# Retention and MLP on one Trainium2 core: the second product of the first block, half of it by seven products, and k of chunks 4 to 7 by casting transfers

## The chip, the cores and the metric

The kernel runs on one core of one Trainium2 chip. The metric is device time in microseconds of one execution, the median of three timed runs. TensorE (PE) multiplies, VectorE (DVE), ScalarE (ACT) and GpSimd (POOL) do the elementwise work, SyncE (SP) issues most transfers; POOL and ACT can issue transfers too.

## The reference

Two layers follow each other: a retention recurrence over 4 batches, 8 heads, 768 tokens and 64 features per head, and a two-layer MLP with Mish on its 3072 tokens of 512 features.

```python
for t in range(S):
    state = gamma[None, :, None, None] * state + np.einsum('bhd,bhe->bhde', k[:, :, t], v[:, :, t])
    y[:, :, t] = scale * np.einsum('bhd,bhde->bhe', q[:, :, t], state)
...
h = x @ w_in                       # 3072 x 512 by 512 x 2048
sp = np.where(h > 20.0, h, np.log1p(np.exp(np.minimum(h, 20.0))))
g = h * np.tanh(sp)
return (g @ w_out).astype(np.float32)   # 3072 x 2048 by 2048 x 512
```

## The kernel before

**Chunks and blocks.** The recurrence is worked in 24 chunks of 128 tokens, six to a batch. For a chunk, PE turns q and k (`turn`, L383, or a transposing transfer, `turn_by_dma`, L363), multiplies them to scores (`scores`, L394), DVE masks them (`mask`, L404), PE adds the masked scores times v (`present`, L463) and the carried state times q (`past`, L457). The state's increment is k times v (`outer_wide`, L445, for chunk 4; `outer`, L411, after that). `y_two` (L506) does present, outer and past of the two chunks of a block, and ACT copies the result to fp16 (`xt`, L516), which is what the MLP of that block starts from. The first block has four chunks (0 to 3), the ten others two each.

**The MLP.** Per block, the first product gives h in PSUM, ACT applies Mish and writes g (fp16), the second product multiplies g by `w_out`. `w_out` comes in four slices of 4 x 128 rows (`FPS` = 4, slices 0 to 3), each 1 MB in fp32; it is cast to fp16 by `cast_wout` (L179). From block 2 on the second product is done by seven half-size products in place of eight (`seven`, L744): sums of g (`sums_a`, L607, and so on) against sums of `w_out` (`weight_sums`, L574, tiles `tmat`, four DVE operations for each half). Block 1 uses seven products in its first product alone. Block 0 uses plain products in both.

**The stage at hand.** `first_block` (L842) runs the recurrence of chunks 0 to 3, then the loop at L936: sixteen steps of the first product (`g1`, L524), then fourteen steps of the second (`g2_mm`, L551), each of which takes one 128-row part of `w_out` for all four token tiles into four PSUM banks (`o_tiles`), and two steps that close the banks (`g2_out`, L557). The dictionary `plan` (L923) hangs the other work on steps of that loop: casts of the `w_out` slices (slices 0, 1 and 2 on DVE, slice 3 on ACT), the recurrence of chunks 4 and 5 (`casts`, `turn`, `scores_one`, `outer_wide`), and `y_two(1)` ahead of the last closing step. `some_late` (L570) takes DVE operations off a list of sums that nothing waits for yet.

**Loads.** Transfers go out in the order of the program on SP's queue: the weights, then q and v of chunk 4, the last quarter of `w_out` in two halves (`load_last_wout`), then q, k and v chunk by chunk (`load_more`, L825; `load_to`). Three loads of chunks 4 and 5 (k of 4, q and v of 5) are issued by ACT instead. Up to chunk 7 (`BRING` = 8) k is loaded as fp32 and cast by ACT (`cast_k`, L346); from chunk 8 on `bring_k` (L340) has POOL issue a transfer that casts to fp16 on its way. POOL scales and casts q and v (`cast_q`, L335; `cast_v`, L350).

**Order.** The order on every engine is the order of the program text (`tc.manual_schedule()`); waits are placed where tiles depend on one another. `gate` (L360) is a one-column POOL copy that makes POOL wait for a tile. `mmps` is a pool of four PSUM banks for the products, `atps` one of two double banks for the recurrence.

Of the kernel before, what the change touches and what calls it, by code (L numbers as in the profile page):

```python
# [9 lines left out]
FP16 = mybir.dt.float16  # L10
# [6 lines left out]
def kernel(  # L17
# [107 lines left out]
    nsnap = [0]  # L125
    SEVEN, HALF_SEVEN = 2, 1
    nload, late = [0], []
    BRING = CPB + 4
    stores = []


# [1 line left out]
    def room(g):  # L133
        loaded[g] = [
            lpool.tile([P, H, D], FP32, name=nm + "f", tag=nm + "f", bufs=6 if nm == "v" else 4)
            if g < BRING or nm != "k" else None for nm in "qkv"]

    def load_one(g, n, queue):
        b, c = divmod(g, NCH)
        queue.dma_start(  # L140
            loaded[g][n], (q, k, v)[n][b, :, c * C:(c + 1) * C].rearrange("h p d -> p h d"))

    def load(g):
        room(g)
        for n in (0, 1, 2) if g < BRING else (0, 2):
            load_one(g, n, nc.sync)

    def load_to(g):
# [27 lines left out]
        eng.tensor_copy(t, src[:, :, half * (TB // 2):(half + 1) * (TB // 2)])  # L176
        wins[s, half] = t

    def cast_wout(s, on_act=False):  # L179
        src = wtmps.pop(("out", s))  # L180
        t = cpool.tile([P, FPS, d_model], FP16, name=f"wout{s}")
        if on_act:
            for f in range(0, FPS, 2):
                nc.scalar.copy(t[:, f:f + 2], src[:, f:f + 2])
        else:
            nc.vector.tensor_copy(t, src)
        wouts[s] = t

    def store(n):
        for _ in range(n):  # L190
# [155 lines left out]
    def cast_k(g):  # L346
        if g < BRING:
            nc.scalar.copy(room16(g)[1], loaded[g][1])

    def cast_v(g):  # L350
        if g < NCK:
            nc.gpsimd.tensor_tensor(  # L352
# [1 line left out]

    def casts(g):
        cast_q(g)
        cast_k(g)
        cast_v(g)

    def gate(x):  # L360
        nc.gpsimd.tensor_copy(gate_t, x)  # L361
# [21 lines left out]
    def turn(g):  # L383
# [7 lines left out]
        nc.vector.tensor_copy(qkt, t_ps)  # L391
        qkts[g] = (qkt[:, :HP], qkt[:, HP:])

    def scores(g):  # L394
# [45 lines left out]
    def state(g):  # L440
        state_sum(g)
        state_decay(g, nc.vector)
        spread_state(g)

    def outer_wide(g):  # L445
        _, k16, v16, _ = cast[g]
        u_ps = u_tile()[:, 0]
        for i in range(HP):
            nc.tensor.matmul(
                u_ps[:, i], k16[:, 2 * i:2 * i + 2], v16[:, 2 * i:2 * i + 2],  # L450
                start=True, stop=True)
        su = stp.tile([P, HP, P], FP32, name="su", bufs=1)
        nc.vector.tensor_tensor(su, u_ps, states[g - 1], op=ALU.add)
        states[g] = stp.tile([P, HP, P], FP16, name="st")
        nc.vector.tensor_tensor(states[g], su, gcm, op=ALU.mult)  # L455

    def past(g, y):  # L457
        st, qt = states[g - 1], qkts[g][0]
# [26 lines left out]
    def outer_state(g):  # L485
        outer(g, u_tile()[:, 0, :, :D])
        state(g)
# [36 lines left out]
    def g1(blk, u):  # L524
        nt = BLOCKS[blk] * C
        per = TB // nt
        h_ps = mmps.tile([P, per, nt], FP32, name="h_ps", tag="mm")
        for j in range(per):
            s, f = divmod(u * per + j, FPS)
            for bp in range(NBP):  # L530
                nc.tensor.matmul(
                    h_ps[:, j], win(s, f, bp), xt(blk, bp),
                    start=(bp == 0), stop=(bp == NBP - 1))
        mish(blk, u, h_ps)
# [35 lines left out]
    def some_late(n):  # L570
        for _ in range(min(n, len(late))):
            late.pop(0)()
# [21 lines left out]

    def room_for_more():
        n, hf = NFB // 2, d_model // 2
        tmats.extend(
            wstage.tile([P, 2, n, hf], FP16, name="tmat", tag="wt", bufs=4) for _ in range(2))

    def sum_views(blk, f=slice(None)):  # L600
        s = gsums[blk % 2]
# [42 lines left out]
    def g1_seven(blk, steps):  # L644
# [54 lines left out]
        def step(name):  # L699
            for fn, *args in steps.get(name, ()):  # L700
                fn(*args)
# [10 lines left out]
        mm(pe, s(1), t(1), True)  # L712
        m5 = snap(pe)
        mish_plain(1, 0, h0)
        step("u2")
        step("p6")
        h1 = plain(3, 0)
        mm(px, s(3), t(3))
# [123 lines left out]
    def first_block():  # L842
# [72 lines left out]
        for s in range(1, NSL):  # L915
# [4 lines left out]
            if s >= 2:  # L920
                some_late(4)
        room_for_sums()
        plan = {  # L923
            9: [(cast_wout, 0)],
            12: [(cast_wout, 1)],
            16: [(cast_wout, 2), (load_more,), (casts, CPB)],
            23: [(casts, CPB + 1), (cast_wout, 3, True)],
            24: [(turn, CPB)],
            25: [(scores_one, CPB)],
            27: [(turn, CPB + 1)],  # L930
            28: [(outer_wide, CPB), (casts, CPB + 2), (turn_and_load, CPB + 2), (cast_q, CPB + 3)],
            29: [(scores_one, CPB + 1)],
            31: [(y_two, 1)],
        }
        o_tiles = [None] * CPB
        for u in range(2, 2 * NFB):  # L936
            if u < NFB:
                g1(0, u)
            elif u < 2 * NFB - 2:
                w = u - NFB  # L940
                for t in range(CPB):
                    if w == 0:
                        o_tiles[t] = mmps.tile([P, d_model], FP32, name="o_ps", tag="mm")
                    g2_mm(o_tiles[t], 0, t, w)
            else:
                for t in range(CPB // 2) if u % 2 == 0 else range(CPB // 2, CPB):
                    for w in range(NFB - 2, NFB):
                        g2_mm(o_tiles[t], 0, t, w)
                    g2_out(o_tiles[t], 0, t, 1, on_act=t == CPB - 1)
            for fn, *args in plan.get(u + 1, ()):  # L950
                fn(*args)
            if u == NFB - 1:
                room_for_more()
                late.extend(weight_sums(0) + weight_sums(1))
            if NFB <= u < NFB + 5:
                some_late(1)
# [46 lines left out]
    def steps_of_half(blk):  # L1003
        a = first[blk] + 4
        return {
            "p2": [(gate_x, blk), (cast_v, a - 1), (bring_k, a)],
            "u2": [(cast_k, a - 1)],
            "p6": [(turn_and_load, a - 1), (some_late, 1)],
            "p7": [(cast_q, a), (some_late, 1)],
            "p4": [(cast_v, a), (bring_k, a + 1), (some_late, 1), (store, 2)],  # L1010
            "end": [(turn_and_load, a), (store, 2)],
        }

    def plan_of(blk):
        a = first[blk] + 4
        return {10: [(scores_two, blk + 1)],
                11: [(cast_q, a + 1)],
                12: [(outer_state, first[blk] + 2), (cast_v, a + 1), (bring_k, a + 2),
                     (turn_and_load, a + 1)],
                14: [(y_two, blk + 1)]}  # L1020

# [56 lines left out]
```

## Time and profile before

| what | value |
|---|---|
| median of 3 runs | 202.63 us (202.52 to 202.92) |
| the profiled execution | 203.19 us, of which the span is 201.3 us |
| PE busy in the span | 192.6 us (96%) |
| DVE, ACT, POOL busy | 138.7, 112.9, 76.9 us |
| granted TensorE clock | 1.00 throughout |
| blocks 2 to 10, each | about 14.6 us (68.0 to 82.6 us is one) |

The span is what the profile covers, from the first to the last instruction; the remaining 1.9 us lie around it. The median of the timed runs is 0.56 us under the profiled execution's own time, so a difference found in the profile is carried to the median, not an absolute time. PE is nearly always busy, so its share says little: what counts is in which stretches PE stands still, and behind what. The stretch that the change touches lies between the last matmul of the first product (32.6 us) and the first of block 1 (51.9 us).

### The profile page before, as it was taken

The page shows a single profiled execution, that of the slowest core. Times are in us where ns is not written, and L with a number is a line of the kernel's source. Part 1 is how long each engine was busy: PE and PEld are TensorE (multiplying, and loading weights), DVE is VectorE, ACT ScalarE, POOL GpSimd, SP SyncE. Part 2 cuts the span into 40 slices and gives each one's busy share as a digit, 9 for nine tenths or more (in the row PEclk, how much of TensorE's full clock was granted, in tenths as well). Part 3 has the DMA queues.
Part 4 walks back from the last instruction along what each step waited for, and adds up shares of the span by engine and source line. Part 5 has one row for each costly group of instructions (what it writes and reads, how often), then busy time and mean ns, then how long its engine had stood idle before and what let it go on. Part 6 is the DMA issues. An engine that isn't in the chain of part 4 may idle for free.

```text
span 201.3 us, 5579 instructions
## 1 busy us (share of the span) xinstructions
PE 192.6 (96%) x2307; PEld 151.6 (75%) x2307; DVE 138.7 (69%) x278; ACT 112.9 (56%) x213; POOL 76.9 (38%) x103
## 2 busy tenths in 40 slices
PE   6987999979999999999999999999999999999993
PEld 2355444445774788988988988988988988988982
DVE  2787594969746559569479587587498597597362
ACT  2462674151780495494584684685664675775750
POOL 7072000617553355645716527618606706100000
PEclk9999999999999999999999999999999999999999
DMA  5999999999989999999998997996999982200202
GB/s 173 301 313 356 384 386 306 265 258 196 156 90 248 254 183 231 179 153 189 136 195 174 196 152 125 187 164 141 192 173 131 168 135 53 107 0 32 77 29 78
DMA packets 95897, 36.57 MB, mean 182 GB/s; under 512 B 82304, under 2 KB 89984, under 8 KB 95872
## 3 DMA queue, kind: packets, MB, share of 16 engines
q1 hardware_dynamic: 75968, 33.30, 74.8%
q0 software_dynamic: 16640, 2.10, 16.5%
q10 hardware_dynamic: 3264, 0.82, 2.4%
q8 instruction: 18, 0.29, 0.6%
q14 instruction: 7, 0.06, 0.1%
HBM read 27.30 MB, written 6.29 MB: 167 GB/s over the span
## 4 chain that ended last, share of the span: by engine, by line
PE 78%; DMA 8%; DVE 8%; ACT 2%; issue 1%; SPq 0%; DVEq 0%
PE o_ps L764 27%; PE h_ps L690 18%; PE h_ps L666 16%; DMA wt<-in_moe_w_out_dram 6%; PE o_ps L553 4%; PE y_ps L469 3%; PE at L400 3%; PE y_ps L460 2%; DMA qfirst<-in_q_dram 2%; PE u_ps L415 1%; DVE tmat L585 1%; ACT xt L516 1%; PE h_ps L838 1%; DVE st L455 1%; DVE tmat L587 1%
## 5 line engine op out<-in xcount | busy, mean ns | idle before, releaser
L690 PE MATMUL h_ps<-xt,win 128*128 128x256 f16 x320 | 41.6, 273 | 0.0
L683 DVE TENSOR_TENSOR hsum<-h_ps,hsnap 128x512 f32<-128x512 f32 x30 | 19.8, 688 | 22.3 <-PE h_ps L666 20.0
L690 PEld LDWEIGHTS <-win 128*128 128x128 f16 x320 | 29.3, 98 | 3.6
L337 POOL TENSOR_TENSOR qk<-qf,qvs 128x512 f16<-128x512 f32 x20 | 21.5, 1077 | 25.8 <-DMA qf<-in_q_dram 25.7
L764 PEld LDWEIGHTS <-gsum 128*128 128x128 f16 x288 | 27.7, 98 | 3.2
L406 DVE TENSOR_TENSOR am<-at,tri 128x1024 f16<-128x1024 f32 x20 | 24.3, 1217 | 3.5 <-PE at L400 3.5
L352 POOL TENSOR_TENSOR v<-vf,qvs 128x512 f16<-128x512 f32 x20 | 23.5, 1173 | 5.1 <-DMA vf<-in_v_dram 5.1
L764 PE MATMUL o_ps<-tmat,gsum 128*128 128x256 f16 x216 | 25.1, 273 | 0.0
L677 ACT ACTIVATE g<-hsum 128x512 f16<-128x512 f32 x30 | 18.5, 631 | 11.0 <-DVE hsum L683 10.9
L697 ACT ACTIVATE g<-h_ps 128x512 f16<-128x512 f32 x40 | 23.0, 603 | 0.7 <-PE h_ps L690 0.6
L764 PEld LDWEIGHTS <-g 128*128 128x128 f16 x216 | 21.0, 98 | 2.5
L553 PE MATMUL o_ps<-wout,g 128*128 128x512 f16 x96 | 22.7, 379 | 0.0
L673 ACT COPY hsnap<-h_ps 128x512 f32<-128x512 f32 x30 | 16.4, 581 | 10.7 <-PE h_ps L666 10.6
L666 PEld LDWEIGHTS <-wsum 128*128 128x128 f16 x320 | 19.5, 98 | 0.5
L778 DVE TENSOR_TENSOR osb<-o_ps,snap 128x256 f32<-128x256 f32 x27 | 11.3, 419 | 11.6 <-PE o_ps L764 10.1
L361 POOL COPY gate<-gsum 128x1 f16<-128x1 f16 x8 | 1.4, 181 | 44.6 <-DVE gsum L738 44.6
L770 ACT COPY snap<-o_ps 128x256 f32<-128x256 f32 x27 | 10.1, 373 | 13.7 <-PE o_ps L764 13.4
L516 ACT CAST xt<-y_ps 128x1024 f16<-128x1024 f32 x10 | 10.1, 1012 | 13.5 <-PE y_ps L460 13.5
L764 PE MATMUL o_ps<-wout,g 128*128 128x256 f16 x144 | 17.2, 273 | 0.0
L666 PE MATMUL h_ps<-xsum,wsum 128*128 128x128 f16 x240 | 16.7, 219 | 0.0
L666 PEld LDWEIGHTS <-win 128*128 128x128 f16 x240 | 15.1, 98 | 1.7 <-issue 1.0
L438 ACT COPY stx<-stc 64x256 f16<-64x256 f16 x30 | 12.0, 400 | 7.5 <-DVE stc L424 5.5
(105 smaller groups left out, 296.9 us busy)
## 6 DMA issues: line engine op xcount, KB each, us to landing
vf<-in_v_dram SPq DMA_DIRECT2D x23, 256.0 KB, 5.7
out_dram<-osb SPq DMA_DIRECT2D x22, 256.0 KB, 5.2
qf<-in_q_dram SPq DMA_DIRECT2D x19, 256.0 KB, 5.0
wt<-in_moe_w_out_dram SPq DMA_DIRECT2D x3, 1024.0 KB, 9.3
wi<-in_moe_w_in_dram SPq DMA_DIRECT2D x4, 512.0 KB, 7.6
wi<-in_moe_w_in_dram SPq DMA_DIRECT2D x2, 1024.0 KB, 11.8
qk<-in_k_dram POOLq DMA_DIRECT2D x16, 128.0 KB, 5.6
kf<-in_k_dram SPq DMA_DIRECT2D x7, 256.0 KB, 5.9
```

The lines of the kernel that those rows point to most:

```text
L337: nc.gpsimd.tensor_tensor(room16(g)[0], loaded[g][0], qs.unsqueeze(2).broadcast_to((P, H, D)), op=ALU.mult)
L352: nc.gpsimd.tensor_tensor(room16(g)[2], loaded[g][2], vs.unsqueeze(2).broadcast_to((P, H, D)), op=ALU.mult)
L406: nc.vector.tensor_tensor(am, ats.pop(g), tri.unsqueeze(1).unsqueeze(1).broadcast_to((P, 2, HP, C)), op=ALU.mult)
L516: nc.scalar.copy(xts[blk][:, :, :2 * C], y_ps.rearrange("p i j c -> p i (j c)"))
L553: nc.tensor.matmul(o_ps, gts[blk, fb][:, t * P:(t + 1) * P], wouts[s][:, f, cols], start=(fb == 0), stop=(fb == NFB - 1))
L666: nc.tensor.matmul(h_ps[:, f], w(f, d), x(d), start=first and f == 0 and d == 0, stop=d == n - 1, skip_group_check=True)
L673: nc.scalar.copy(x, h_ps)
L677: nc.scalar.activation(gt[:, 2 * i * FPS:(2 * i + 1) * FPS, j * P:(j + 1) * P], h, AF.Mish, scale=inv_boost3)
L683: nc.vector.tensor_tensor(h, h_ps, x, op=ALU.add)
L690: nc.tensor.matmul(h_ps[:, j], win(s, 2 * half + j, bp), xt(blk, bp), start=bp == 0, stop=bp == NBP - 1)
L697: nc.scalar.activation(gt[:, fb:fb + 2], h_ps, AF.Mish, scale=inv_boost3)
L764: nc.tensor.matmul(o_ps, x(f), w(f), start=first and f == 0, stop=f == n - 1, skip_group_check=True)
```

## The change

The loop over sixteen second-product steps is replaced by a new function `first_g2`. It treats the tokens of block 0 as two pairs of tiles, and of the four slices of `w_out` it multiplies slices 0 and 2 by seven products in place of eight (with the sums of `weight_sums(0)`, now made here, and four sums of g in `gsum`), slices 1 and 3 plainly. Slice 3 comes last for all tiles (`end`). Accumulators of a pair share two PSUM banks; partial results are copied out by ACT (into `osb` and `snap`) while the bank goes on accumulating. Slice 2 is cast half by DVE and half by ACT, slice 3 by ACT as before; the copies of turned q and k (`turn`) move from DVE to ACT. `outer_wide` is split, its second DVE operation (`decay_wide`) placed after the mask of chunk 5.

`BRING` goes from 8 to 4: k of chunks 4 to 7 comes by `bring_k`, issued by POOL, and the ACT casts of k and the fp32 loads of k are gone. All q and v loads of chunks 4 and 5 are on SP, ahead of the last quarter of `w_out`.

```diff
-    BRING = CPB + 4
+    BRING = CPB
...
-    def cast_wout(s, on_act=False):
+    def cast_wout(s, on_act=0):
...
+        n = FPS - on_act
+        if n:
+            nc.vector.tensor_copy(t[:, :n], src[:, :n])
+        for f in range(n, FPS, 2):
+            nc.scalar.copy(t[:, f:f + 2], src[:, f:f + 2])
...
-        load_one(CPB, 0, nc.sync)
-        load_one(CPB, 2, nc.sync)
+        for g in (CPB, CPB + 1):
+            load_one(g, 0, nc.sync)
+            load_one(g, 2, nc.sync)
     def load_more():
-        load_one(CPB, 1, nc.scalar)
-        load_one(CPB + 1, 0, nc.scalar)
-        load_one(CPB + 1, 2, nc.scalar)
-        load_one(CPB + 1, 1, nc.sync)
         load_last_wout(0)
         load_last_wout(1)
...
+        plan = {9: [(cast_wout, 0), (room_for_more,), (bring_first,)],
+                10: [(some_late, 1)], 13: [(cast_wout, 1), (room_for_more,)], 16: [(load_more,)]}
+        late.extend(weight_sums(0) + weight_sums(1))
+        for u in range(2, NFB):
+            g1(0, u)
             for fn, *args in plan.get(u + 1, ()):
                 fn(*args)
+        first_g2()
...
+    def bring_first():
+        gate(wtmps["out", 1][:, 0, :1])
+        bring_k(CPB)
+        bring_k(CPB + 1)
+
+    def first_g2():
...
+        for p in pairs:
+            mm(px[p], a(p, 0, 0), b(0, 0), True)
+            nc.scalar.copy(osb[p][0][:, 0], px[p])
+        g_sum(1, g_part(0, 1), g_part(2, 1), ALU.add)
+        g_sum(2, the_sum(1), g_part(0, 0), sub)
+        for p in pairs:
+            mm(pz[p], a(p, 1, 1), b(1, 1))
+        for p in pairs:
+            mm(pe[p], sm(p, 1), t(1), True)
+            nc.scalar.copy(m5[p], pe[p])
+        cast_wout(2, FPS // 2)
+        some_late(1)
+        gate(tmats[0][:, 1, 0, :1])
+        casts(CPB)
+        bring_k(CPB + 2)
+        some_late(1)
+        g_sum(3, g_part(0, 0), g_part(0, 1), sub)
+        g_sum(4, g_part(2, 0), the_sum(2), sub)
+        some_late(1)
+        for p in pairs:
+            mm(pb[p], a(p, 0, 1), b(1, 0))
+        for p in pairs:
+            mm(pb[p], a(p, 0, 2), b(2, 0))
+        for p in pairs:
+            mm(pe[p], a(p, 0, 1), b(1, 1))
+        for p in pairs:
+            mm(px[p], sm(p, 2), t(2))
+            nc.scalar.copy(osb[p][0][:, 1], px[p])
+        turn(CPB, True)
+        for p in pairs:
+            mm(px[p], sm(p, 3), t(3))
+            nc.vector.tensor_tensor(osb[p][1][:, 1], px[p], m5[p], op=ALU.add)
+        casts(CPB + 1)
+        bring_k(CPB + 3)
+        for p in pairs:
+            mm(pe[p], sm(p, 4), b(2, 1))
+        scores_one(CPB)
+        turn(CPB + 1, True)
+        cast_wout(3, FPS)
+        for p in pairs:
+            mm(px[p], a(p, 1, 2), t(4))
+        for p in pairs:
+            mm(px[p], a(p, 1, 1), b(1, 0))
+        outer_wide(CPB)
+        casts(CPB + 2)
+        turn_and_load(CPB + 2)
+        cast_q(CPB + 3)
+        scores_one(CPB + 1)
+        decay_wide(CPB)
+
+        def end(p, i):
+            mm((t0, t1)[i][p], a(p, i, 3), lambda f: wouts[3][:, f], last=True)
+            if i == 0:
+                nc.vector.tensor_tensor(osb[p][0], t0[p], osb[p][0], op=ALU.add)
+            else:
+                nc.vector.tensor_tensor(osb[p][1][:, 1], pz[p], osb[p][1][:, 1], op=ALU.add)
+                nc.scalar.copy(osb[p][1][:, 0], px[p])
...
+        end(0, 0)
+        end(0, 1)
+        end(1, 0)
+        y_two(1)
+        end(1, 1)
```

In the shorthand of `first_g2`, `a(p, i, s)` is g of token tile 2p+i and slice s, `b(s, j)` column half j of slice s of `w_out`, `sm(p, i)` and `t(i)` the sums of g and of `w_out`; each `mm` is four matmuls of 256 columns (512 in `end`). `px` and `pz` are the halves of one PSUM tile of the pair (`t1`), `pb` and `pe` those of the other (`t0`).

More of the change, by code (lines that the diff above doesn't have):

```diff
@@ L135, in room @@
             lpool.tile([P, H, D], FP32, name=nm + "f", tag=nm + "f", bufs=6 if nm == "v" else 4)
-            if g < BRING or nm != "k" else None for nm in "qkv"]
+            if nm != "k" else None for nm in "qkv"]
     def load_one(g, n, queue):
@@ L144, in load @@
         room(g)
-        for n in (0, 1, 2) if g < BRING else (0, 2):
+        for n in (0, 2):
             load_one(g, n, nc.sync)
@@ L177, in cast_win @@
         wins[s, half] = t
-    def cast_wout(s, on_act=False):
+    def cast_wout(s, on_act=0):
         src = wtmps.pop(("out", s))
[L181 to L187, printed above, removed]
+        t = wouts[s] = cpool.tile([P, FPS, d_model], FP16, name=f"wout{s}")
+        n = FPS - on_act
[3 more added lines that the diff above has]
+            nc.scalar.copy(t[:, f:f + 2], src[:, f:f + 2])
     def store(n):
@@ L344, in bring_k @@
                 room16(g)[1], k[b, :, c * C:(c + 1) * C].rearrange("h p d -> p h d"))
-    def cast_k(g):
-        if g < BRING:
-            nc.scalar.copy(room16(g)[1], loaded[g][1])
     def cast_v(g):
@@ L356, in casts @@
         cast_q(g)
-        cast_k(g)
         cast_v(g)
@@ L381, in spin_wide, with turn @@
             tri.unsqueeze(1).broadcast_to((P, n, C)), start=True, stop=True)
-    def turn(g):
+    def turn(g, on_act=False):
         q16, k16 = cast[g][:2]
@@ L390, in turn @@
         qkt = qktp.tile([P, H, C], FP16, name="qkt", bufs=4)
-        nc.vector.tensor_copy(qkt, t_ps)
+        if on_act:
+            nc.scalar.copy(qkt, t_ps)
+        else:
+            nc.vector.tensor_copy(qkt, t_ps)
         qkts[g] = (qkt[:, :HP], qkt[:, HP:])
@@ L451, in outer_wide, with decay_wide @@
                 start=True, stop=True)
-        su = stp.tile([P, HP, P], FP32, name="su", bufs=1)
-        nc.vector.tensor_tensor(su, u_ps, states[g - 1], op=ALU.add)
+        sus[g] = stp.tile([P, HP, P], FP32, name="su", bufs=1)
+        nc.vector.tensor_tensor(sus[g], u_ps, states[g - 1], op=ALU.add)
+    def decay_wide(g):
         states[g] = stp.tile([P, HP, P], FP16, name="st")
-        nc.vector.tensor_tensor(states[g], su, gcm, op=ALU.mult)
+        nc.vector.tensor_tensor(states[g], sus.pop(g), gcm, op=ALU.mult)
     def past(g, y):
@@ L483, in u_tile @@
         return atps.tile([P, 2, HP, P], FP32, name="u_ps", tag="at")
-    def outer_state(g):
-        outer(g, u_tile()[:, 0, :, :D])
-        state(g)
     def handed_on(blk):
@@ L596, in room_for_more @@
         n, hf = NFB // 2, d_model // 2
-        tmats.extend(
-            wstage.tile([P, 2, n, hf], FP16, name="tmat", tag="wt", bufs=4) for _ in range(2))
+        tmats.append(wstage.tile([P, 2, n, hf], FP16, name="tmat", tag="wt", bufs=4))
     def sum_views(blk, f=slice(None)):
@@ L714, in g1_seven @@
         mish_plain(1, 0, h0)
-        step("u2")
         step("p6")
@@ L922, in first_block @@
         room_for_sums()
[L923 to L949, printed above, removed]
+        plan = {9: [(cast_wout, 0), (room_for_more,), (bring_first,)],
+                10: [(some_late, 1)], 13: [(cast_wout, 1), (room_for_more,)], 16: [(load_more,)]}
@@ L950, in first_block @@
+        late.extend(weight_sums(0) + weight_sums(1))
+        for u in range(2, NFB):
+            g1(0, u)
             for fn, *args in plan.get(u + 1, ()):
                 fn(*args)
[L952 to L956, printed above, removed]
-        hsnaps.append(gp.tile([P, 4, TB], FP32, name="hsnap", tag="g0"))
+        first_g2()
+        hsnaps.append(gp.tile([P, 4, TB], FP32, name="hsnap", tag="g0"))
@@ new lines, in bring_first, with a, sm, b @@
+    def bring_first():
[3 more added lines that the diff above has]
+    def first_g2():
+        hf = d_model // 2
+        sub = ALU.subtract
+        pairs = range(CPB // 2)
+        t1 = [mmps.tile([P, 2, hf], FP32, name="o_ps", tag="mm") for _ in pairs]
+        t0 = [mmps.tile([P, 2, hf], FP32, name="o_ps", tag="mm") for _ in pairs]
+        osb = [[op.tile([P, 2, hf], FP32, name="osb", tag="osb") for _ in range(2)] for _ in pairs]
+        m5 = [op.tile([P, hf], FP32, name="snap", tag="snap", bufs=3) for _ in pairs]
+        pb, pe = [t[:, 0] for t in t0], [t[:, 1] for t in t0]
+        px, pz = [t[:, 0] for t in t1], [t[:, 1] for t in t1]
+        sums = gsums[0].rearrange("p s (f a) t -> p s f (a t)", a=2)
+        def a(p, i, s):
+            return lambda f: gts[0, s * FPS + f][:, (2 * p + i) * P:(2 * p + i + 1) * P]
+        def sm(p, i):
+            return lambda f: sums[:, i - 1, f, p * P:(p + 1) * P]
+        def b(s, j):
+            return lambda f: wouts[s][:, f, j * hf:(j + 1) * hf]
+        def t(i):
+            return lambda f: tmats[(i - 1) // 2][:, (i - 1) % 2, f]
+        def mm(o_ps, x, w, first=False, last=False):
+            for f in range(FPS):
+                nc.tensor.matmul(
+                    o_ps, x(f), w(f), start=first and f == 0, stop=last and f == FPS - 1,
+                    skip_group_check=True)
+        def g_part(s, i):
+            g = gtiles[0, s // 2][:, s % 2 * FPS:(s % 2 + 1) * FPS]
+            return g.rearrange("p f (a i t) -> p f a i t", a=2, i=2)[:, :, :, i]
+        def g_sum(dst, x, y, f):
+            d = sums[:, dst - 1].rearrange("p f (a t) -> p f a t", a=2)
+            nc.vector.tensor_tensor(d, x, y, op=f)
+        def the_sum(i):
+            return sums[:, i - 1].rearrange("p f (a t) -> p f a t", a=2)
+        for p in pairs:
[51 more added lines that the diff above has]
+                nc.vector.tensor_tensor(osb[p][0], t0[p], osb[p][0], op=ALU.add)
+            else:
+                nc.vector.tensor_tensor(osb[p][1][:, 1], pz[p], osb[p][1][:, 1], op=ALU.add)
+                nc.scalar.copy(osb[p][1][:, 0], px[p])
+            row0 = (2 * p + i) * P
+            stores.append((1, out[row0:row0 + P], osb[p][i].rearrange("p j c -> p (j c)")))
+        end(0, 0)
[3 more added lines that the diff above has]
+        end(1, 1)
@@ L1017, in plan_of @@
                 11: [(cast_q, a + 1)],
-                12: [(outer_state, first[blk] + 2), (cast_v, a + 1), (bring_k, a + 2),
+                12: [(state, first[blk] + 2), (cast_v, a + 1), (bring_k, a + 2),
                      (turn_and_load, a + 1)],
```

1 line of the change is left out of this document (removed).

## Prediction

> **What bounds the kernel now.** First the page's busy shares, then the busy time by stage, then PE, ACT, DVE and POOL in order of time through the stretch that changes.
>
> ```profile
> span 201.3 us, 5579 instructions
> ...
> PE 192.6 (96%) x2307; PEld 151.6 (75%) x2307; DVE 138.7 (69%) x278; ACT 112.9 (56%) x213; POOL 76.9 (38%) x103
> ```
>
> ```profile
> core 0: us, PE busy (x) PEld busy (x) DVE busy (x) ACT busy (x) POOL busy (x), PEclk, DMA share, GB/s
> 32.60:51.80 19.20, 17.84 (x134) 8.85 (x133) 15.19 (x16) 5.67 (x9) 8.48 (x7) 1.00 1.17 236
> 39.70:43.00 3.30, 2.27 (x24) 1.20 (x23) 2.80 (x5) 1.35 (x2) 1.40 (x1) 1.00 1.18 308
> ...
> 68.00:82.60 14.60, 14.60 (x199) 13.15 (x199) 10.80 (x24) 9.61 (x19) 7.73 (x10) 1.00 1.43 213
> ```
>
> From 68 us on PE has no gap, so whatever moves the start of block 1 moves the end by as much. Between 32.6 and 51.8 us PE stands still for 1.36 us, 1.03 of it between 39.7 and 43.0, while the transfers never rest (share above 1). The lines of that stretch:
>
> ```profile
> 33.01 0.60 ACT L547 ACTIVATE g<-h_ps 128x512 f16<-128x512 f32 x1 [0.27 <-PE h_ps L531]
> ...
> 34.98 1.23 DVE L186 CAST wout<-wt 128x2048 f16<-128x2048 f32 x1 [1.58 <-DMA wt<-in_moe_w_out_dram]
> 36.13 0.68 DVE L585 TENSOR_TENSOR tmat<-wout 128x1024 f16<-128x1024 f16 x1
> ...
> 36.22 1.50 POOL L337 TENSOR_TENSOR qk<-qf,qvs 128x512 f16<-128x512 f32 x1 [19.64 <-DMA qf<-in_q_dram]
> 36.84 1.42 DVE L586 TENSOR_TENSOR tmat<-wout,tmat 128x1024 f16<-128x1024 f16 x1
> 37.68 1.49 POOL L352 TENSOR_TENSOR v<-vf,qvs 128x512 f16<-128x512 f32 x1
> ...
> 42.42 0.40 PE L400 MATMUL at<-qkt 64*128 64x128 f16 x8 [1.03 <-DVE qkt L391]
> ...
> 43.98 1.04 ACT L184 CAST wout<-wt 128x1024 f16<-128x1024 f32 x1 [0.66 <-DMA wt<-in_moe_w_out_dram]
> ...
> 48.35 1.04 POOL L352 TENSOR_TENSOR v<-vf,qvs 128x512 f16<-128x512 f32 x1 [0.41 <-DMA vf<-in_v_dram]
> ...
> 50.81 1.01 ACT L516 CAST xt<-y_ps 128x1024 f16<-128x1024 f32 x1 [3.12 <-PE y_ps L460]
> ...
> 51.87 1.05 PE L666 MATMUL h_ps<-xt,win 128*128 128x128 f16 x16 [0.24 <-ACT xt L516]
> ```
>
> The reader is to see three things. A sum on DVE and a cast on POOL that overlap take about 1.45 us each instead of 0.68 and 1.04. PE's long wait is for `qkt`, whose copy stood behind DVE's sums. And v of chunk 6 lands as late as 48.3 us; its cast ends (49.39) 0.5 us before `y_two` needs it (outer product, 49.85).
>
> **What the change removes.** PE: 64 matmuls of 512 columns become 88 of 256 and 16 of 512, that is 2048 columns fewer. Sixteen of 256 take 1.75 us in the chain of waits (0.109 each, 0.217 for 512), so 0.87 us. ACT loses four k casts of 0.62 us (2.5), one after 52 us. DVE loses two qkt copies (1.4), half a cast (0.6) and the plain output copies. None of it is worth its own length: the stage ends by chains of waits, which the change re-lays.
>
> **What it adds.** ACT gets eight copies of 128x256 (0.37 each by L770; two fall in the tail), two qkt copies (1.01 by L226, the nearest row) and half a slice (1.04 by L184). DVE gets four sums of g (0.68 each, the shape of L585), two adds of 0.42 and heavier closing adds; one more sum of `w_out` stays over for block 1, where DVE is idle for 1.8 of 6.6 us: nothing, or 0.7 us if that cover were gone. POOL gets two gates (0.18) and four k issues (0.94 to 1.07 by L343).
>
> **The new chain, step by step**, from the last Mish (33.61), on the change's program order; most steps are one after another because PSUM tiles are shared.
> - ACT copies px of both pairs, 2 x 0.37: 34.35. Only then may PE write pz, in the same bank as px. Last pz, then pe of both, 12 matmuls x 0.109 plus 0.16 to the last one's end: 35.8.
> - ACT copies the second m5 (0.37: 36.2), then casts its half of slice 2 (landed 34.98; 1.04): 37.25. DVE's second sum of `w_out` (0.68): 37.95. POOL's gate (0.18): 38.15.
> - POOL: q and v of chunk 4, colliding with DVE's sums, 1.50 and 1.49: 41.1. Issue of k of chunk 6, 0.94: 42.1. q of chunk 5, 1.04: 43.1.
> - PE turns chunk 5, 8 x 0.055 plus 0.16: 43.7. ACT copies qkt: 44.7, then both halves of slice 3: 46.8. Landing of slice 3: 34.98, plus six chunk loads (q, v and k of 4 and 5), plus the 2.81 us of a slice (34.98 less 32.17, the landings of slices 2 and 1). A chunk load is (48.3 - 34.98 - 2.81)/9 = 1.17 us, nine having landed in that time. That makes 44.8, so the casts wait for ACT, not for the transfer.
> - PE: the last two matmuls of `end(0, 0)`, then eight for two more tiles, 10 x 0.217: 49.0. `y_two`: 1.44 us in the steady stage (79.69 to 81.13), less 0.2 for eight outer matmuls that this one lacks: 50.2. xt, 1.01, and 0.1 around it: 51.3.
> - Some twelve hand-overs between engines of 0.02 to 0.05 us (41.68 + 0.68 to 42.42 is 0.06) add 0.3: block 1 starts at 51.6 against 51.87, 0.27 us earlier.
>
> PE is not the bound of this chain; its own work in the stage (9.6 + 3.5 + 2.9 us of recurrence from 32.8 on) would end near 48.8. `y_two` also needs v of chunk 6: the same nine loads and slice 3 go ahead of and with it, so it lands at 48.3 again and is cast by 49.4, about when PE reaches the outer product (49.0 + 0.5). That is a tie.
>
> **Casting transfers.** The page gives 16640 packets at 16.5% of 16 engines, 31.9 ns a packet; ACT's queue, fp32 loads, 3264 at 2.4%, 23.7 ns. A k load of 1024 packets so costs 2.04 against 1.52 us of all engines, at most 0.5 us more; against the mean of the main queue (31.7 ns) nothing. I take 0.1, as the difference of landings with packets overlapping is 1.17 a chunk; bounds 0 and 0.5 each, 1.5 us for k of 4, 5 and 6 if all went into v of chunk 6. From issue to landing such a load takes 5.6 us (the median of section 6): k of 4, issued at 32.4 behind its gate, lands near 38.0, of 5, issued at 33.4, near 39.0; PE turns them once q is cast, at 39.7 and 43.1. Cover: 1.7 and 4.1 us. On SP, q and v of 5 now stand ahead of slice 3's last quarter, which is the six loads counted above.
>
> POOL issues k of 4 and 5 while DVE casts slice 1 (32.17 to 33.40), and no row here shows an issue against such a cast; against a two-input sum (53.80, 0.87 instead of 0.68) it took 1.07. Bounds: no delay, or all of the 1.23 us. I take no effect, since either stays inside the cover. The Trainium skill, "SBUF — State Buffer", section "SBUF: two separate sides", says a DVE cast out of fp32 in SBUF locks GpSimd out, so that it cannot write descriptors until the cast ends, and speaks against this placing. By it both k loads slip by about 1 us, and the sum stays the same; no run here shows it yet.
>
> **Rivals.**
> 1. *Faster: the POOL chain is shorter and the loads come sooner.* q and v of 4 at 1.04 each save 0.9 us; k of 6, issued at 41 us, falls behind v of 6 on the rings, which then lands at 47.1 and no longer binds. The block starts 0.9 to 1.1 us earlier than before: 201.6. For: the fewer DVE sums in flight when v of 4 is cast. Against: four sums follow the gate directly.
> 2. *Slower: v of chunk 6 comes late.* k of 7 is now issued at about 44.2 us, ahead of the end of v of 6, where it used to stand behind q of 7. If the engines take turns between queues, one chunk load (1.17 us) slips in front: landing 49.5, cast to 50.5, outer and past 0.8: 51.3, xt: 52.4 and hand-overs 52.6, 0.7 to 0.9 us later: 203.4. It decides as soon as v of 6 lands after 48.4 us. For: k of chunk 9 (POOL, 57.14) and q of 8 (SP, 57.87) landed at 63.2 and 63.4, as good as together. Against: between 36 and 41 us the loads of SP and ACT landed one by one. The Trainium skill, "DMA: Bandwidth & Descriptors", section "Queues, rings and completion order", has each engine go round the queues; by it this rival is the case, and the traces bear it out in the first of these pairs alone.
> 3. *The casting transfers starve.* The longest of them took 7.1 us (65.53 to 72.58). With that and the 1.23, k of 4 lands at 40.7, whose wait PE makes up before q of 5 is cast, and k of 5 at 41.7, in time. Only beyond 43.1 does it move the chain, one for one; at 43.9 that is 0.8 us: 203.2.
> That the saved matmuls buy nothing, as they turn into waits, is not a rival but the forecast.
>
> **How the numbers follow.** The profiled execution is 203.19 us with a span of 201.3; the median is 202.63. Taking 0.27 off the median: 202.4, within 0.2% (0.4 us, about what a measurement here can tell from no change). Chances: forecast 0.38, rival 1 0.33, rival 2 0.22, rival 3 0.07. Of the forecast's 0.38, a spread of 0.4 us around its sum leaves 0.28 within 0.2%, 0.07 faster, 0.03 slower. Together faster 0.40, same 0.28, slower 0.32. The range runs from a little past rival 1 (201.4) to rival 2 (203.5); the likeliest case alone holds 202.0 to 202.8.
>
> **What would show it.** Right: PE's first matmul of block 1 between 51.2 and 52.0; its waits in the stage behind ACT (px copies, slice 3), not DVE's qkt; POOL's casts of chunk 4 at 1.4 to 1.5 us; gap-free blocks from then on. Wrong: the cast of v of chunk 6 starting after 48.5 us and PE waiting for it (rival 2), casts of chunk 4 at 1.04 and a start before 51 (rival 1), PE waiting for k of 4 or 5 (rival 3), or a new gap inside block 1.

## The result: 0.73% slower, and the profile after

The changed kernel takes 204.26 us, the median of four runs (204.22 to 204.31), against 202.77 (202.52 to 203.03) for the kernel before: a ratio of 1.0073, with a 95% interval of 1.0058 to 1.0089. The forecast of 202.4 missed by 1.9 us, and the time lies above its range. Times and ratios leave out three slow executions of the run with the casting transfers alone, which took 205.93 to 206.1 us at a granted clock of 0.99. A ratio is an estimate of its own, not the quotient of two medians.

The page of the changed kernel, its first lines:

```profile
span 202.5 us, 5658 instructions
...
PE 192.0 (95%) x2339; PEld 155.4 (77%) x2339; DVE 139.9 (69%) x283; ACT 115.8 (57%) x219; POOL 82.5 (41%) x109
```

The span has grown by 1.2 us. PE is busy for 0.6 us less and stands still for longer.

Busy time by stretch, first the changed kernel (the stage, block 1, block 2), then block 1 of the kernel before. The columns are those shown with the prediction: the stretch, its length, then each engine.

```profile
31.60:51.68 20.08, 18.48 (x179) 13.06 (x177) 14.36 (x19) 9.77 (x16) 13.47 (x13) 1.00 1.35 226
51.68:68.91 17.23, 15.67 (x172) 10.73 (x172) 10.32 (x17) 8.04 (x15) 8.64 (x9) 1.00 1.37 205
68.91:83.50 14.59, 14.59 (x199) 13.17 (x199) 10.78 (x24) 9.49 (x19) 7.73 (x10) 1.00 0.88 162
```

```profile
51.87:67.95 16.08, 15.84 (x180) 10.79 (x180) 8.42 (x16) 8.46 (x16) 8.07 (x9) 1.00 1.06 175
```

The first row starts 1.0 us ahead of the stage. From 32.6 us on PE works for 17.48 of 19.08 us; before, it worked for 17.84 of the 19.27 us up to 51.87. The stage has 0.36 us less work and 0.17 us more standstill. It ends at 51.68, where 51.6 was forecast. The loss is in block 1, which the forecast took as unchanged: 17.23 us in place of 16.08, with less PE work in it (15.67 against 15.84) and a standstill of 1.56 us in place of 0.24.

The timeline of the changed kernel through the stage and block 1; each row is start, length, engine, line, operation, and in brackets the idle time before it and what ended that:

```profile
32.94 0.60 ACT L542 ACTIVATE g<-h_ps 128x512 f16<-128x512 f32 x1 [0.27 <-PE h_ps L526]
33.43 0.75 ACT L971 COPY osb<-o_ps 128x256 f32<-128x256 f32 x2
...
36.06 1.05 ACT L186 CAST wout<-wt 128x1024 f16<-128x1024 f32 x1
...
37.14 0.69 DVE L581 TENSOR_TENSOR tmat<-wout,tmat 128x1024 f16<-128x1024 f16 x1 [1.71 <-ACT wout L186]
...
38.44 1.50 POOL L336 TENSOR_TENSOR qk<-qf,qvs 128x512 f16<-128x512 f32 x1
39.91 1.48 POOL L347 TENSOR_TENSOR v<-vf,qvs 128x512 f16<-128x512 f32 x1
...
44.06 1.01 ACT L386 COPY qkt<-t_ps 128x1024 f16<-128x1024 f16 x1 [2.40 <-PE t_ps L383]
44.97 1.99 ACT L186 CAST wout<-wt 128x1024 f16<-128x1024 f32 x2
47.02 1.04 POOL L347 TENSOR_TENSOR v<-vf,qvs 128x512 f16<-128x512 f32 x1 [0.33 <-DMA vf<-in_v_dram]
...
50.62 1.01 ACT L511 CAST xt<-y_ps 128x1024 f16<-128x1024 f32 x1 [0.67 <-PE y_ps L459]
51.68 1.05 PE L660 MATMUL h_ps<-xt,win 128*128 128x128 f16 x16 [0.24 <-ACT xt L511]
...
60.98 0.40 PE L397 MATMUL at<-qkt 64*128 64x128 f16 x8
61.42 1.22 DVE L403 TENSOR_TENSOR am<-at,tri 128x1024 f16<-128x1024 f32 x1 [1.56 <-PE at L397]
62.70 0.40 PE L397 MATMUL at<-qkt 64*128 64x128 f16 x8 [1.32 <-DVE am L403]
64.88 0.41 DVE L421 TENSOR_TENSOR stc<-u_ps,gcv 128x256 f16<-128x256 f32 x1
68.91 1.05 PE L660 MATMUL h_ps<-xt,win 128*128 128x128 f16 x16 [0.24 <-ACT xt L511]
```

The same work in block 1 of the kernel before:

```profile
61.17 0.62 PE L400 MATMUL at<-qkt 64*128 64x128 f16 x16
61.61 2.36 DVE L406 TENSOR_TENSOR am<-at,tri 128x1024 f16<-128x1024 f32 x2 [3.00 <-PE at L400]
63.56 0.32 PE L415 MATMUL u_ps<-v,qk 128*64 128x64 f16 x8
```

The reader is to see the scores (`at`). Before, PE wrote those of chunks 6 and 7 in one go, sixteen matmuls. After, it writes eight, stands still for 1.32 us until DVE has masked them, and writes the other eight. The cause is an edit that neither the diff shown above nor the prediction speaks of: in `plan_of`, step 12 of block 1, `outer_state` for chunk 6 has become `state`. The old one computed chunk 6's outer product k times v a second time, into a fresh PSUM tile (the eight matmuls at 63.56), and so `y_two(1)` gave its own tile of outer products back at once. The new one reads the product that `y_two(1)` left at 50 us. That tile is one of the two double banks of `atps`, and it is held until `stc`, at 64.88, has read it. Until then all scores share the other bank, and those of chunk 7 wait for the mask of chunk 6.

From the start of block 2 to the start of DVE's last copy both kernels take 130.20 us:

```profile
198.15 0.42 DVE L776 COPY osb<-o_ps 128x256 f32<-128x256 f32 x1 [0.45 <-PE o_ps L764]
```

```profile
199.11 0.42 DVE L769 COPY osb<-o_ps 128x256 f32<-128x256 f32 x1 [0.45 <-PE o_ps L757]
```

The span ends 3.15 us behind that start before (201.3 - 198.15) and 3.39 after (202.5 - 199.11). So the two profiled spans differ by -0.19 (stage), +1.15 (block 1), 0.00 (blocks 2 to 10) and +0.24 (the close): 1.20 us. The whole times of these two executions differ by 1.12 us (204.31 against 203.19). The medians differ by 1.49, since the profiled execution of before was 0.42 us slower than its median (203.19 against 202.77) and that of after 0.05 (204.31 against 204.26).

### The profile page after: what moved, and what is told of

Same layout as the page of the kernel before. It is cut to its first block, busy times and chain, and to the rows that moved or that the text cites. A ratio compares the mean times of both kernels' runs of the same rounds, so it can differ in the third digit from the quotient of the medians.

```text
span 202.5 us, 5658 instructions
## 1 busy us (share of the span) xinstructions
PE 192.0 (95%) x2339; PEld 155.4 (77%) x2339; DVE 139.9 (69%) x283; ACT 115.8 (57%) x219; POOL 82.5 (41%) x109
## 4 chain that ended last, share of the span: by engine, by line
PE 84%; ACT 5%; DVE 3%; POOL 2%; DMA 2%; issue 2%; DVEq 0%; POOLq 0%
PE o_ps L757 27%; PE h_ps L684 18%; PE h_ps L660 16%; PE h_ps L526 6%; PE o_ps L548 3%; PE y_ps L468 3%; PE at L397 3%; PE y_ps L459 2%; DMA qfirst<-in_q_dram 2%; PE o_ps L954 2%; ACT wout L186 1%; POOL qk L336 1%; PE h_ps L828 1%; ACT xt L511 1%; PE u_ps L412 1%
## 5 line engine op out<-in xcount | busy, mean ns | idle before, releaser
L342 POOL DMA_DIRECT2D qk<-in_k_dram x20 | 18.8, 942 | 0.0
```

The lines of the kernel that those rows point to most:

```text
L342: nc.gpsimd.dma_start(room16(g)[1], k[b, :, c * C:(c + 1) * C].rearrange("h p d -> p h d"))
```

## The experiments

The theory: the loss is the held tile. The rivals: the stage or the casting transfers are the cause. The kernel before took 202.79 us beside the first four kernels (the median of 25 runs) and 202.99 beside the next four (11 runs).

**The outer product again.** The changed kernel with `outer_state` put back.

```diff
+    def outer_state(g):
+        outer(g, u_tile()[:, 0, :, :D])
+        state(g)
...
-                12: [(state, first[blk] + 2), (cast_v, a + 1), (bring_k, a + 2),
+                12: [(outer_state, first[blk] + 2), (cast_v, a + 1), (bring_k, a + 2),
```

> The changed kernel, but chunk 6's outer product is computed a second time in block 1, into a PSUM tile of its own, as the kernel before does (the changed kernel keeps the tile of y_two(1) in use until state(6), after the masks). Theory A (the kept tile leaves one of the two double banks for the scores of chunks 6 and 7, so that scores of 7 wait for the mask of 6): the 1.32 us wait at 62.70 is gone, block 1 takes 16.1 us as before instead of 17.2, less 1.15 us in all: 203.1 us (202.7 to 203.3), no slower than the kernel before by more than 0.2%. Rival B (the loss comes from the new stage itself, and the wait in block 1 only shows it): 204.0 to 204.4, with another wait of about 1 us in the same block.

Measured: 203.49 us (203.1 to 203.78, 7 runs), ratio 1.0023 (1.0011 to 1.0034).

```profile
60.95 0.62 PE L397 MATMUL at<-qkt 64*128 64x128 f16 x16
...
67.73 1.05 PE L664 MATMUL h_ps<-xt,win 128*128 128x128 f16 x16 [0.24 <-ACT xt L515]
```

The sixteen scores stand together again and block 1, from 51.65, takes 16.08 us as before. The wait goes with the held tile. The time lies above the range expected, 202.7 to 203.3: without the wait the rest of the change is still a little slower than the kernel before. The seven runs lie in two groups, three at 203.10 to 203.14, with the profiled one, and four at 203.49 to 203.78.

**The tile kept, alone.** The kernel before with this one edit.

```diff
-                12: [(outer_state, first[blk] + 2), (cast_v, a + 1), (bring_k, a + 2),
+                12: [(state, first[blk] + 2), (cast_v, a + 1), (bring_k, a + 2),
```

> The kernel before, with the second outer product of chunk 6 taken out, so that state(6) reads the tile of y_two(1): the one edit of the change in block 1, alone. Theory A: scores of chunk 7 wait for the mask of chunk 6, 1.3 us, block 1 takes 17.2 us instead of 16.1: 203.9 us (203.6 to 204.2). Rival B: eight matmuls fewer, 0.2 us faster or the same: 202.5 to 202.8.

Measured: 203.97 us (203.82 to 204.46, 5 runs), ratio 1.0057 (1.0043 to 1.007).

```profile
51.45 1.05 PE L666 MATMUL h_ps<-xt,win 128*128 128x128 f16 x16 [0.24 <-ACT xt L516]
62.47 0.40 PE L400 MATMUL at<-qkt 64*128 64x128 f16 x8 [1.32 <-DVE am L406]
68.67 1.05 PE L666 MATMUL h_ps<-xt,win 128*128 128x128 f16 x16 [0.24 <-ACT xt L516]
```

The one word makes the wait of 1.32 us and a block of 17.22 us. Alone it costs 0.57%, where the whole change costs 0.73%. The first row carries a second lesson: with the stage of the kernel before, block 1 began at 51.45 here, not at 51.87. Slice 2 was cast from 34.54 on instead of 34.98, while Mish ran no earlier. The stage before hangs on landings, and these moved by 0.44 us between two executions.

**The state early.** The changed kernel, `state` of chunk 6 moved ahead of the scores, so that the tile is free when they need it, with no second outer product.

```diff
-        return {10: [(scores_two, blk + 1)],
+        return {8: [(state, first[blk] + 2)],
+                10: [(scores_two, blk + 1)],
...
-                12: [(state, first[blk] + 2), (cast_v, a + 1), (bring_k, a + 2),
+                12: [(cast_v, a + 1), (bring_k, a + 2),
```

> The changed kernel with state(6) moved from the twelfth step of block 1's loop to the eighth, ahead of the scores of chunks 6 and 7: the kept tile is read and free before the second scores need it, and the second outer product stays out. Theory A: the 1.32 us wait is gone and the 0.2 us of the second outer product with it: 202.9 us (202.6 to 203.2), 1.2 to 1.5 under the changed kernel. Rival B: 204.0 to 204.4.

Measured: 202.86 us (202.63 to 203.25, 11 runs), ratio 1.0005 (0.9995 to 1.0016).

```profile
60.94 0.62 PE L397 MATMUL at<-qkt 64*128 64x128 f16 x16
...
67.37 1.05 PE L660 MATMUL h_ps<-xt,win 128*128 128x128 f16 x16 [0.24 <-ACT xt L511]
```

Block 1, from 51.64, takes 15.73 us: 0.35 us less than before, the second outer product, and 1.50 less than in the changed kernel. So `state` alone would have been a gain; where it was put it costs 1.50 and saves 0.35. Without its wait the change is worth nothing either way.

**The casting transfers alone**, in the kernel before.

```diff
-    BRING = CPB + 4
+    BRING = CPB
...
-            9: [(cast_wout, 0)],
+            9: [(cast_wout, 0), (bring_first,)],
...
-            16: [(cast_wout, 2), (load_more,), (casts, CPB)],
-            23: [(casts, CPB + 1), (cast_wout, 3, True)],
+            16: [(cast_wout, 2), (load_more,), (casts, CPB), (bring_k, CPB + 2)],
+            23: [(casts, CPB + 1), (bring_k, CPB + 3), (cast_wout, 3, True)],
```

> The kernel before with the second part of the change alone: k of chunks 4 to 7 by casting transfers issued by POOL, q and v of 4 and 5 on SP ahead of the last quarter of w_out, no ACT casts of k. The second product of block 0 stays plain. Theory (that chain of waits is DVE's: slice 2, sums, qkt copies; k lands in time; v of chunk 6 lands about 47 instead of 48.2): 202.4 to 203.0, the same as before. Rival (casting transfers cost transfer time that the stage lacks): block 1 starts 0.5 to 1 us later, 203.3 to 203.8.

Measured: 203.67 us (202.72 to 205.38, 9 runs), ratio 1.0033 (1.0005 to 1.006). The runs lie in groups: four at 202.72 to 202.78, as expected, three at 204.14 to 204.16, to which the profiled one belongs, and one each at 203.67 and 205.38.

```profile
38.77 2.05 DVE L582 TENSOR_TENSOR tmat<-wout,wout 128x1024 f16<-128x1024 f16 x1
```

```profile
43.52 0.40 PE L395 MATMUL at<-qkt 64*128 64x128 f16 x8 [1.90 <-DVE qkt L386]
```

A sum of 0.68 us takes 2.05 on DVE while POOL issues k of chunk 6 (38.24) and casts q of chunk 5 (39.20); the qkt copy stands behind DVE's sums, and PE waits 1.90 us for it. Block 1 starts at 52.66, 0.79 us later than before. The median and this start are the rival's numbers, but the transfers were not late: v of chunk 6 landed at 46.95, as the theory had it. This is inconclusive: in that order of work the casting loads can cost over a microsecond, in this execution by a collision of POOL and DVE. Only one execution has a profile, so what picks the group is open.

**Seven products alone, k loaded as before.** The state early, k of chunks 4 to 7 as fp32 loads cast by ACT, three of them issued by ACT.

```diff
-    BRING = CPB
+    BRING = CPB + 4
...
     def load_more():
+        load_one(CPB, 1, nc.scalar)
+        load_one(CPB + 1, 0, nc.scalar)
+        load_one(CPB + 1, 2, nc.scalar)
+        load_one(CPB + 1, 1, nc.sync)
```

> The first part of the change alone, with state(6) early as in e3: the second product of block 0 by first_g2, but k of chunks 4 to 7 loaded as fp32 and cast by ACT, and k of 4, q and v of 5 issued by ACT, as in the kernel before. Theory (the chain of the stage runs through ACT's copies of px, m5 and its half of slice 2): ACT's three issues stand in front of the px copies and take 3.9 us in the profile of before (33.08 to 37.06), so the chain from the px copies on starts about 3.6 us later, less what the waits of the later steps give back; block 1 starts 2.5 to 3.6 us after 51.6, 205.2 to 206.5 us. Rival (the stage is bound by the transfers, ACT has room): within 0.5 us of e3, 202.4 to 203.4.

Measured: 206.52 us (205.29 to 207.33, 6 runs), ratio 1.0163 (1.0136 to 1.019).

```profile
33.06 0.41 ACTq L140 DMA_DIRECT2D kf<-in_k_dram  x1
33.51 0.59 ACTq L140 DMA_DIRECT2D qf<-in_q_dram  x1
34.14 2.82 ACTq L140 DMA_DIRECT2D vf<-in_v_dram  x1
37.01 0.65 ACT L980 COPY osb<-o_ps 128x256 f32<-128x256 f32 x2 [3.42 <-DMA kf<-in_k_dram]
37.43 1.86 PE L963 MATMUL o_ps<-wout,g 128*128 128x256 f16 x8 [3.60 <-ACT osb L980]
```

```profile
PEclk9999999589999999999999999999999999999999
```

ACT's three issues last until 37.0, and the px copies that free PE's bank stand behind them: at 37.01 in place of 33.43. That shows why the loads had to leave ACT's queue. The median lies at the upper end of what was expected, and block 1 starts later than expected, at 56.42, because PE lost more than the delay: after its standstill of 3.60 us the granted clock is 0.50 from 37.4 to 43.0 us (the two low digits of the second view, which has 40 slices of the span), and the eight matmuls of the row at 37.43 take 1.86 us, where eight take 1.04 at the full clock. The two runs whose mean clock was 0.998 and 0.999 took 205.57 us or less. The run tells nothing of the seven products; a later one does.

**Shortening the chain.** By the chain of the forecast two edits should move block 1 forward, once block 1 itself is mended. Slice 2 whole on DVE (on top of the state early):

```diff
-        cast_wout(2, FPS // 2)
+        cast_wout(2)
```

> e3 with all of slice 2 cast by DVE (1.23 us from its landing at 34.55) instead of half by ACT, which in the changed kernel only starts at 36.06, behind the copies of px and m5. Theory (ACT's half of slice 2 sets the second sum of w_out, that sets POOL's gate, q and v of 4 and 5, the turns and the casts of slice 3): the sum ends near 36.6 instead of 37.8, all after it moves up by about 1.2 us, block 1 starts at 50.4 to 50.8: 201.8 us (201.5 to 202.3). Rival (transfers bind: v of chunk 6 lands at 46.9, k of 6 at 47.7): no gain, 202.6 to 203.1.

Measured: 202.02 us (201.68 to 202.11, 6 runs), ratio 0.9953 (0.994 to 0.9965), inside the range expected.

And q of chunk 5 cast by POOL ahead of the issue of k of 6 (on top of the state early):

```diff
         casts(CPB)
+        cast_q(CPB + 1)
         bring_k(CPB + 2)
...
-        casts(CPB + 1)
+        cast_v(CPB + 1)
```

> e3 with POOL casting q of chunk 5 ahead of issuing k of chunk 6 and of casting v of chunk 5. Theory: q of 5 is ready 0.95 us earlier, so the turn of 5, its copy and ACT's casts of slice 3 end 0.85 us earlier (46.1 instead of 46.96), block 1 starts near 50.8: 202.0 us (201.8 to 202.4). Rival: k of chunk 6, issued 1.06 us later, lands about 48.7 and the outer product of y_two(1) waits for it: 202.6 to 203.1.

Measured: 202.3 us (202.07 to 202.5, 6 runs), ratio 0.997 (0.9958 to 0.9982), inside the range too.

Both together:

> e7 and e8 together. Theory: 1.2 and 0.85 us do not add up, as slice 3 lands at 44.4 and v of 6 is cast at 48.1 at the earliest; block 1 starts at 49.9 to 50.3: 201.3 us (201.0 to 201.8), faster than both kernels. Rival (transfers bind): 202.4 to 203.1.

Measured: 201.87 us (201.48 to 202.19, 6 runs), ratio 0.9949 (0.9936 to 0.9962); it beats both kernels, and lies just above the range expected. Block 1 starts at 50.94, 51.14 and 50.69 in the three, against 51.64, each 0.1 to 0.4 us later than its forecast. The gains add up to less than their sum, and the timeline of the last shows where:

```profile
42.86 1.01 ACT L386 COPY qkt<-t_ps 128x1024 f16<-128x1024 f16 x1 [1.62 <-PE t_ps L383]
43.77 2.21 ACT L186 CAST wout<-wt 128x1024 f16<-128x1024 f32 x2
```

```profile
46.03 2.32 PE L954 MATMUL o_ps<-wout,g 128*128 128x512 f16 x10 [0.37 <-ACT wout L186]
```

ACT reaches slice 3 at 43.77, but its second half lands at 44.91 only: the pair of casts takes 2.21 us in place of 1.99. The two gains of 0.70 and 0.50 us give 0.95 together, and these 0.22 us are most of what is missing. The chain of engines has met the transfer.

**Seven products alone, all loads on SP.** The state early and fp32 loads of k, all issued by SP; then the same with the two edits that shorten the chain. The kernel before took 202.66 us beside them (21 runs). The first differs from the run with ACT's three issues in these lines:

```diff
-        load_one(CPB, 1, nc.scalar)
-        load_one(CPB + 1, 0, nc.scalar)
-        load_one(CPB + 1, 2, nc.scalar)
+        load_one(CPB, 1, nc.sync)
+        load_one(CPB + 1, 0, nc.sync)
+        load_one(CPB + 1, 2, nc.sync)
```

> The changed kernel with the state of chunk 6 early, but k of chunks 4 to 7 again as fp32 loads cast by ACT, all of them issued by SP in the order q4, v4, k4, q5, v5, k5, slice 3. Theory A (the way in which k comes is worth nothing in the stage; kernels with the casting loads end about 0.25 us later behind their last landing, 1.0 against 1.25 to 1.3 us in the traces so far): block 1 starts at 51.4 to 51.9, the rest behind the last landing 1.0 to 1.1 us, 202.6 (202.3 to 203.0) against 202.86 with casting loads. Theory B (the casting loads carry a gain in the stage, since ACT is rid of its casts and SP's queue of four loads): block 1 starts after 52.0, over 203.1. Theory C (the casting loads cost transfer time, the prediction's rival): slice 3 and v of chunk 6 land over 0.5 us earlier, block 1 starts before 51.2, under 202.3.

> The same with slice 2 cast whole by DVE and q of chunk 5 cast ahead, the two edits that brought 201.87 with casting loads. Theory A: 201.6 (201.3 to 202.0), block 1 from 50.7. Theory B: over 202.1. Theory C: under 201.3.

Measured: 202.72 us (202.22 to 203.56, 11 runs), ratio 1.0006 (0.9993 to 1.0019), and 202.39 (202.13 to 202.67, 11 runs), ratio 0.9986 (0.9977 to 0.9995). PE in the first, and in the second:

```profile
49.66 0.32 PE L417 MATMUL u_ps<-v,qk 128*64 128x64 f16 x8 [0.68 <-POOL v L347]
...
51.63 1.05 PE L665 MATMUL h_ps<-xt,win 128*128 128x128 f16 x16 [0.24 <-ACT xt L516]
```

```profile
42.70 0.40 PE L388 MATMUL t_ps<-ident,qk 128*128 128x128 f16 x4 [0.81 <-ACT qk L352]
...
49.60 0.32 PE L417 MATMUL u_ps<-v,qk 128*64 128x64 f16 x8 [0.63 <-POOL v L347]
```

The time of the first agrees with theory A, the reason only in part. With every load on SP, where k of chunk 6 also stands ahead of it, v of chunk 6 lands at 48.4 us, against 46.9 by the changed kernel's two queues, and PE now waits for it. In the second k of chunk 5 (landed 42.0) and v of chunk 6 (48.35) take nearly the whole gain of the two edits in the stage: block 1 starts at 51.57 against 51.63. The median of 202.39 is theory B's number. It still lies 0.33 us under the first, which the two profiles do not explain. So the casting loads do carry something in the stage, 1.5 us of landing, which comes to bear only where the engines are early enough. And they come with a price at the end: from the last landing to the end of the span it is 1.0 us here and in the kernel before, and 1.3 in the kernels with casting loads for chunks 4 to 7. Neither part showed a gain by itself: the seven products with all loads on SP and the state early are the same as the kernel before.

## Why the prediction was wrong

**The step that failed** is the sentence "From 68 us on PE has no gap, so whatever moves the start of block 1 moves the end by as much". It carries a gain from the start of block 1 to the end of the kernel, past a block in which the change had an edit of its own. That block has its gaps before 68 us, and the edit makes a new one: +1.50 us of wait and -0.35 of saved outer product, shown from both sides by the kernel before with this edit alone (+0.57%) and by the changed kernel without it. The working costs the edits in the stage one after another and leaves out the one in `plan_of`. The list of what would prove it wrong ended with "a new gap inside block 1", which is what came, but no rival put a price on it: the term stood at nothing, and measured 1.15 us.

**The sum of the stage was right**, but for the transfers. The first column gives the end of each step as forecast, the second as the trace has it.

| step | forecast | measured |
|---|---|---|
| ACT's px copies | 34.35 | 34.18 |
| ACT's half of slice 2 | 37.25 | 37.11 |
| DVE's second sum of `w_out` | 37.95 | 37.83 |
| POOL's gate | 38.15 | 38.48 |
| q and v of chunk 4 | 41.1 | 41.39 |
| second qkt copy | 44.7 | 45.07 |
| slice 3 cast | 46.8 | 46.96 |
| last two of `end(0, 0)` and two more tiles | 49.0 | 49.34 |
| xt | 51.3 | 51.63 |
| block 1 starts | 51.6 | 51.68 |

The only term of the table that was off by a multiple is the gate, 0.18 forecast, 0.50 measured: it ended at 38.48, with the sum on DVE (38.43) that it met. The lag that it opens stays to the end (0.33 at xt), where the 0.3 that the forecast adds for hand-overs covers it. Beside the table, the forecast had v of chunk 6 land at 48.3 again, and it landed at 46.9; the tie with PE that the forecast names was none, since the cast ended at 48.06 and PE reached the outer product at 49.74.

**The gain of 0.27 was within what the stage before varies by.** It was taken against a block 1 that began at 51.87. In the run of the kernel before with the tile kept it began at 51.45, at that kernel's median time. Against such an execution the new stage is 0.2 us slower. With the close of the span, +0.24, that would cover the 0.35 us by which the profiled run of the changed kernel with the outer product again (203.14) lies above the median of the kernel before (202.79); no profile of an execution at that median was taken, so this is not shown. Why the median of that changed kernel is 203.49 stays open. The new stage did not follow that landing: in the three profiled executions that have it unaltered, with casting loads, block 1 began at 51.68, 51.65 and 51.64, though slice 2 was cast from 34.97 on in the second and from 34.57 on in the others.

**Rival 1** (a shorter POOL chain) did not happen in its first half: q and v of chunk 4 took 1.50 and 1.48, as the forecast had it. Its second half did: k of chunk 6 landed behind v of chunk 6, which no longer bound; but the chain of engines ended later, so nothing was gained. **Rival 2** (v of chunk 6 late) did not either. It landed at 46.9, not at 49.5. Its mechanism may be there, though: k of chunk 6, issued by POOL from 41.3 to 42.3, landed at 47.7, ahead of q of chunk 7, whose issue by SP lasted from 40.0 to 44.1 and which landed at 48.8. The Trainium skill, "DMA: Bandwidth & Descriptors", section "Queues, rings and completion order", has each engine go round the queues. These rows agree with that, but do not show it alone, since SP's issue ended after POOL's. What was wrong is on whom the turn falls: v of chunk 6 was issued from 38.1 on in the changed kernel, and from 41.4 on where k of 4, 5 and 6 stand ahead of it on SP's queue, and it moved up by more than the other queue took away. **Rival 3** gave 203.2 for starving loads; k of 4 and 5 landed at 38.2 and 39.8, inside their cover (38.0 and 39.0 forecast).

**The issue of k under a DVE cast.** DVE's cast of slice 1, and POOL's gate and two issues in the changed kernel:

```profile
31.75 1.23 DVE L184 CAST wout<-wt 128x2048 f16<-128x2048 f32 x1 [0.65 <-DMA wt<-in_moe_w_out_dram]
```

```profile
31.78 1.24 POOL L355 CAST gate<-wt 128x1 f16<-128x1 f32 x1 [15.18 <-DMA wt<-in_moe_w_out_dram]
32.96 1.95 POOL L342 DMA_DIRECT2D qk<-in_k_dram  x2
```

The gate, of one column, ends with DVE's cast, and the issues begin there, 1 us later than a gate of 0.18 would let them. The Trainium skill, "SBUF — State Buffer", section "SBUF: two separate sides", has a DVE cast out of fp32 lock GpSimd out; by that rule both loads slip by about 1 us. Both issues began that much later, with the sum unmoved as forecast. What met the cast was the gate in front of the issues; the issues themselves came after it, so no run here shows an issue that starts under such a cast. DVE is slowed as well: its cast of half of slice 2, which met the end of these issues, took 0.86 us, and 0.69 in the kernel where k is loaded by SP and POOL is at rest.

## What to carry to other kernels

Cost every hunk of a change, the shortest most of all: an operation that computes something a second time may be there to give a buffer back, and where a pool has two buffers, holding one across a stage makes the writers of the other wait for their readers. A gain at one point reaches the end only if each stage in between keeps its length; look at the change's own edits there before carrying it on. A gain smaller than the spread of the stage it is read from (here 0.4 us between two executions) is no forecast, however well the sum is worked.

## What was not expected of the hardware

- A one-column POOL copy took 0.18 us alone, 0.50 beside a two-input sum on DVE and 1.24 under DVE's cast out of fp32: in both cases it ended within 0.05 us of the DVE operation that it met.
- After PE stood still for 3.60 us in the run with ACT's three issues, the granted clock was 0.50 for 5.6 us (37.4 to 43.0).
- Kernels with casting loads of chunks 4 to 7 end 1.26 to 1.29 us behind their last landing, those without 1.01 to 1.04 (seven kernels and five; three of the five have the rest of the change). What in the close takes the 0.25 us was not tried.
- The landings in the stage before moved by 0.44 us between two executions of the same stage (slice 2 at 34.54 and 34.98), with its matmuls in place.
